# Placed dummies, u in its own bank, x copied by two engines and a last group with tokens on partitions, in a sketched attention with an MLP behind it

## The chip, the core and the metric

The kernel runs on one core of a Trainium2 chip. The core has TensorE (PE, matmuls; PEld is its weight loads), VectorE (DVE), ScalarE (ACT), GpSimd (POOL) and SyncE (SP), each with its own instruction stream, joined by semaphores. DMAs are issued from the streams of SyncE and ScalarE. The metric is device time in microseconds (us) of one execution, as the median of several; lower is better. The profile of one execution gives its span, from the first to the last instruction, on which all times below are counted.

## What is computed

```python
# q, k, v: (4, 4, 1088, 32), S1, S2: (8, 32), w_in: (128, 2048), w_out: (2048, 128)
def phi(x):                                   # 64 features of a token
    a = einsum('rd,bhsd->bhsr', S1, x)
    b = einsum('rd,bhsd->bhsr', S2, x)
    return einsum('bhsi,bhsj->bhsij', a, b).reshape(..., 64)
q_p, k_p = phi(q), phi(k)
kv  = einsum('bhsf,bhsd->bhfd', k_p, v)
z   = sum(k_p, axis=2)
num = einsum('bhsf,bhfd->bhsd', q_p, kv)
den = einsum('bhsf,bhf->bhs', q_p, z)[..., None] + 1e-06
x   = (num / den).transpose(0, 2, 1, 3).reshape(4352, 128)
h   = x @ w_in
out = (h - tanh(h)) @ w_out                   # (4352, 128)
```

There is no softmax: the sums over the keys of a batch (kv and z) are small matrices, and each token of q is weighed with them. Since h − tanh(h) is linear in its first part, the kernel computes the output as x @ (w_in @ w_out) + tanh(−h) @ w_out, with w_in @ w_out kept as two bf16 matrices, whi and wlo.

## The kernel before, in words

A small planner (class Program) takes all operations with their reads, writes, costs and priorities, and writes out one order for each engine; semaphore waits follow from it. An operation of the MLP has a due time (`due`, from FIRST, TILE, EARLY; matmuls by w_out LAG later), and earlier operations get theirs by counting back with the costs stretched by STRETCH. So constants such as LAG, TILE, STRETCH, HELD, HOT and LATE change nothing but the order. For the opening (batch 0), the dictionary LINE fixes the order of the named operations on each engine (lines 52 to 59), and other operations fall between them where the planner puts them.

**Opening, batch 0.** Two tiny DMAs bring S1 and S2, ScalarE's queue brings k, SyncE's the first half of q and v. `warm` offers dummies, which multiply a tile of zeros into PSUM bank 6: 36 (BURN) of 128 columns and 60 of 512; the planner puts them where TensorE has nothing ready, until the matmuls of line 840. `sketch` (L569) spreads S; VectorE makes from it the masked weights wkm (L572), wqb's first part wab (L576) and wab2 (L580). k is transposed on VectorE in 32x32 blocks into kT (L600, four pieces) and projected (keys0, keys1, L618); ScalarE copies the projections (kab, L628), and VectorE and GpSimd multiply them into features wk (L650, L636). `spread` (L585) and s2c (L588) prepare the second sketch; `gram` (L666), gm (L695) and `fold` (L704) make a small matrix, from which VectorE writes wqb's second part wu (L715). q of the first 512 tokens (chunk a) is projected in two steps: `qab` with the first 16 columns of wqb and `qu` with the last 8, both into PSUM bank 1 (L773). ScalarE copies qab's part (ab, L798). VectorE multiplies u with ab (au, L802), reduces it to the denominator (dn, L805), inverts it (rd, L808), scales (an, L810), multiplies out the features (qp, L819; the other half on GpSimd, L814), and transposes them (qpT, L825, two pieces). `sums` (L676) are kv, copied to kvz (L728), turned (L734) and copied to ndw (L739); `nd0` and `nd1` (L840) weigh qpT with ndw into banks 4 to 7, and line 854 copies the result, cast to bf16, to xT.

**Weights.** w_in comes in four DMAs, issued by SyncE once the first kab is there, w_out in two, once wu is there. They are cast to bf16 on ScalarE (w_in 0 to 2) and GpSimd (w_in 3 and w_out). w_in is transposed on TensorE (L875) and multiplied with w_out (L889) for whi and wlo.

**The other chunks.** The remaining 576 tokens of batch 0 (chunk c, projection `qc`) and then batches 1 to 3, of 1088 tokens each, go the same way (L784, L707 in place of L773, L704), between the MLP's matmuls. Loads of batch 1 wait for GATE1, those of later batches for GATES of the batch before.

**MLP.** The tokens are cut into eight groups of 512 and one of 256. For each of 16 blocks of w_in, a matmul (L918) writes h of the group, transposed, into one of PSUM banks 4 to 6; ScalarE writes tanh(−h) to one of 40 slots of tt (L921); a matmul by w_out (L929) adds it up in bank 7, with whi and wlo (L910) in the same sum. VectorE transposes the sum in 32x32 blocks into osb (L936), and four DMAs, one for each 32 columns of the output, write it out in rows of 128 bytes (L945), from SyncE; in the last group two of them from ScalarE.

## Time and profile before

| what | value |
|---|---|
| time, median of 3 runs | 108.56 us (108.46 to 108.84) |
| time of the profiled execution | 108.72 us |
| its span | 106.9 us |
| TensorE matmuls busy | 99.4 us (93%) |
| ScalarE busy | 76.5 us (72%), of it 70.2 us tanh |
| VectorE, GpSimd busy | 61.1 us, 23.9 us |
| first matmul of the MLP (L918) | 17.61 us |
| x of batch 3 there, last run of tanh begins | 80.89 us |
| transpose of the last group | 103.74 us |

Busy times are sums over instructions; matmuls are pipelined, so their busy time holds some overlap. The chain of waits follows back, from the last instruction, what released each step, or the instruction ahead of it on its engine. A timeline line gives start, length, engine, line, operation, and the idle time before it with what ended it.

### The profile page before, as it was taken

To read this page: it belongs to the slowest core of one execution; us is meant where nothing else is said; L and a number is where in the kernel's file an instruction comes from. 1 tells how busy PE (TensorE), PEld (TensorE's weight loads), DVE (VectorE), ACT (ScalarE), POOL (GpSimd) and SP (SyncE) were. 2 spreads that over 40 slices of the span, in tenths; PEclk is the share of its full clock that TensorE was granted. 3 is DMA by queue.
4 is the path that set the end of the run, shared out by engine and by line. 5 is a ranking of instruction groups with operands and counts; after the bars stand their busy time and mean duration, and the time that the engine had idled before them with its cause. 6 is when DMAs were issued, how large, how long until landed. Compare 5 with 4: busy or idle time off the path is not lost.

```text
span 106.9 us, 3548 instructions
## 1 busy us (share of the span) xinstructions
PE 99.4 (93%) x1534; PEld 56.6 (53%) x1552; DVE 61.1 (57%) x119; ACT 76.5 (72%) x160; POOL 23.9 (22%) x34
## 2 busy tenths in 40 slices
PE   5999999999999999999999999999999999999970
PEld 5967657445566544536465446544644344345650
DVE  3672797996389987734999914486935100200210
ACT  3012174997168964996978698679777999999960
POOL 5517076400531600620430005308000000000000
PEclk9999999999999999999999999999999999999997
DMA  3987899920024793600189613300132041023153
GB/s 58 348 209 213 287 291 294 297 63 0 6 35 69 238 323 74 96 3 6 13 326 266 94 38 47 51 6 0 23 49 32 0 71 27 6 42 57 17 84 49
DMA packets 25247, 11.24 MB, mean 105 GB/s; under 512 B 18832, under 2 KB 23440, under 8 KB 25232
## 3 DMA queue, kind: packets, MB, share of 16 engines
q1 hardware_dynamic: 24400, 10.40, 40.3%
q10 hardware_dynamic: 832, 0.62, 2.2%
q8 instruction: 12, 0.20, 0.8%
q14 instruction: 3, 0.02, 0.1%
HBM read 8.79 MB, written 2.23 MB: 103 GB/s over the span
## 4 chain that ended last, share of the span: by engine, by line
PE 81%; ACT 12%; issue 3%; DVE 1%; DVEq 0%
PE ps L929 23%; PE ps L918 23%; ACT tt L921 11%; PE ps L565 7%; PE ps L840 6%; PE ps L910 4%; PE ps L618 4%; PE ps L784 4%; PE ps L676 3%; PE ps L773 2%; DVE osb L936 1%; PE ps L875 1%; PE ps L666 1%; PE ps L889 1%; PE ps L734 1%
## 5 line engine op out<-in xcount | busy, mean ns | idle before, releaser
L921 ACT ACTIVATE tt<-ps 128x512 bf16<-128x512 f32 (+1 forms) x144 | 70.2, 594 | 11.6 <-PE ps L918 6.5
L918 PE MATMUL ps<-xT,w_in 128*128 128x512 bf16 (+1 forms) x135 | 47.5, 367 | 1.5 <-issue 1.0
L929 PE MATMUL ps<-tt,w_out 128*128 128x512 bf16 (+1 forms) x139 | 44.4, 367 | 0.3 <-issue 0.3
L918 PEld LDWEIGHTS ps<-xT,w_in 128*128 128x128 bf16 x144 | 13.4, 97 | 16.3 <-ACT tt L921 5.4
L929 PEld LDWEIGHTS ps<-tt,w_out 128*128 128x128 bf16 x144 | 13.9, 98 | 14.1 <-issue 1.2
L936 DVE STREAM_TRANSPOSE osb<-ps 128x512 f32<-128x512 f32 (+1 forms) x9 | 6.2, 684 | 23.1 <-PE ps L929 23.1
L636 POOL TENSOR_TENSOR wk<-kab 128x512 f32<-128x512 f32 (+1 forms) x8 | 9.4, 1180 | 28.5 <-ACT kab L628 28.0
L814 POOL TENSOR_TENSOR qp<-an,ab 128x1152 f32<-128x1152 f32 (+2 forms) x5 | 8.9, 1778 | 19.4 <-DVE an L810 19.4
L825 DVE STREAM_TRANSPOSE qpT<-qp 128x1152 f32<-128x1152 f32 (+2 forms) x10 | 11.0, 1112 | 0.1
L565 PE MATMUL ps<-wz 128*128 128x128 bf16 (+1 forms) x47 | 7.4, 334 | 1.4 <-DVE hmask L532 1.2
L840 PE MATMUL ps<-qpT,ndw 32*32 32x288 f32 (+3 forms) x320 | 7.0, 352 | 0.0
L854 DVE CAST xT<-ps 128x512 bf16<-128x512 f32 x8 | 5.2, 687 | 3.1 <-PE ps L840 3.0
L650 DVE TENSOR_TENSOR wk<-ps,kab 128x512 f32<-128x512 f32 (+1 forms) x8 | 5.8, 740 | 0.7 <-ACT kab L628 0.7
L600 DVE STREAM_TRANSPOSE kT<-kraw 128x256 f32<-128x256 f32 (+3 forms) x10 | 5.7, 600 | 0.6 <-DMA kraw<-in_k_dram 0.6
L565 PEld LDWEIGHTS ps<-wz 128*128 128x128 bf16 x50 | 4.9, 135 | 2.0 <-DVE hmask L532 1.2
L628 ACT COPY kab<-ps 128x320 f32<-128x320 f32 (+1 forms) x5 | 2.1, 419 | 5.4 <-PE ps L618 5.4
L618 PEld LDWEIGHTS ps<-wkm,kT 128*64 128x64 f32 x144 | 4.8, 141 | 2.0 <-DVE xT L854 0.8
L618 PE MATMUL ps<-wkm,kT 128*64 128x64 f32 x144 | 5.4, 229 | 0.3 <-issue 0.3
L819 DVE TENSOR_TENSOR qp<-an,ps 128x1152 f32<-128x1152 f32 (+2 forms) x5 | 5.6, 1114 | 0.2
L840 PEld LDWEIGHTS ps<-qpT,ndw 32*32 32x32 f32 x320 | 4.0, 103 | 3.2 <-DVE qpT L825 1.0
L746 DVE STREAM_TRANSPOSE qT<-qraw 128x512 f32<-128x512 f32 (+3 forms) x9 | 5.6, 651 | 0.0
L798 DVE COPY ab<-ps 128x576 f32<-128x576 f32 x3 | 2.3, 758 | 5.2 <-PE ps L784 5.2
(72 smaller groups left out, 71.1 us busy)
## 6 DMA issues: line engine op xcount, KB each, us to landing
kraw<-in_k_dram SPq DMA_DIRECT2D x3, 544.0 KB, 4.1
qraw<-in_q_dram SPq DMA_DIRECT2D x3, 544.0 KB, 5.6
out_dram<-osb SPq DMA_DIRECT2D x20, 64.0 KB, 2.0
w_in_f<-in_moe_w_in_dram SPq DMA_DIRECT2D x4, 256.0 KB, 4.3
w_out_f<-in_moe_w_out_dram SPq DMA_DIRECT2D x2, 512.0 KB, 5.4
vx<-in_v_dram SPq DMA_DIRECT2D x6, 144.0 KB, 5.4
vx<-in_v_dram SPq DMA_DIRECT2D x6, 128.0 KB, 5.4
vx<-in_v_dram SPq DMA_DIRECT2D x6, 64.0 KB, 2.8
```

Source lines behind the costliest of these rows:

```text
L565: P.op("tensor", cost, lambda e: e.matmul(ps[:, 6, 0:cols], wz[:, 0:128], wz[:, 0:cols], start=True, stop=True), r=[("wz",)], prio=prio)
L600: P.op("vector", dve(hi - lo), lambda e, cb=cb, t0=t0, n=n, lo=lo, hi=hi: e.transpose(out=kT[i][:, t0:t0 + n, cb:cb + 2, :], in_=kraw[i][: ...
L618: ins = e.matmul(dst[64 * c:64 * c + 64, :, :, t - t0, :], kT[i][:, t, 2 * c:2 * c + 2, :].rearrange("p c j -> p (c j)"), wkm[:, :, :, :]. ...
L636: P.op("gpsimd", pool(64 * n), lambda e, t0=t0, t1=t1, n=n, ab_=ab_: e.tensor_tensor(out=wk[:, 1, t0:t1, :, :].rearrange("p t h (i j) -> p ...
L650: P.op("vector", dve(64 * n), lambda e, t0=t0, t1=t1, n=n, a_ps=a_ps, b_sb=b_sb: e.tensor_tensor(out=wk[:, 0, t0:t1, :, :].rearrange("p t ...
L814: P.op("gpsimd", pool(64 * n), lambda e: e.tensor_tensor(out=qp[u][:, 1, 0:64 * n].rearrange("p (n i j) -> p n i j", i=R, j=R), in0=an[u][ ...
L825: c.t_op = P.op("vector", dve(64 * n), lambda e, r=r: e.transpose(out=qpT[u][:, r, 0:64 * n], in_=qp[u][:, r, 0:64 * n]), r=[("qp", u, r)] ...
L840: ins = e.matmul(ps[32 * h:32 * h + 32, k0 + s, 0:32 * own[s]], ndw[b % 2][32 * s:32 * s + 32, y, 32 * h:32 * h + 32], src, start=(y == 0) ...
L918: P.op("tensor", pe(n), lambda e, jb=jb, bk=bk: e.matmul(bk[:, 0:n], w_in[:, 128 * jb:128 * jb + 128], xT[:, t0:t0 + n], start=True, stop= ...
L921: P.op("scalar", act(n), lambda e, ts=ts, bk=bk: e.activation(out=tt[:, ts, 0:n], in_=bk[:, 0:n], func=AF.Tanh, scale=-1.0), r=[kb], w=[(" ...
L929: P.op("tensor", pe(n), lambda e, jb=jb, ts=ts: e.matmul(acc[:, 0:n], w_out[:, jb, :], tt[:, ts, 0:n], start=(jb == 0 and not g), stop=(jb ...
L936: P.op("vector", dve(n), lambda e: e.transpose(out=osb[u][:, 0:n], in_=acc[:, 0:n]), r=[ka], w=[("osb", u)], want=due(NJB) + LAG)
```

## The change

The diff, cut to its core. Planner constants whose lines are left out: BIAS (0 to 10), HOT (4000 to 3900), HELD (ScalarE added), STRETCH (TensorE and ScalarE 1.8 to 1.3, GpSimd 1.6 to 1).

```diff
-LAG = 8000
-TILE = 760
+LAG = 6000
+TILE = 680
-COPY_K = ("scalar", "scalar", "vector")
+COPY_K = ("scalar", "vector", "vector")
-COPY_Z = "vector"
+COPY_Z = "scalar"
-W_PRIO = 22
-BURN = 36
+W_PRIO = 26
-X_A = "vector"
-ORD = 3
+X_A = "vector", "scalar"
+ORD = 2
-C_ENG = "scalar", "scalar", "scalar", "gpsimd"
-GATES = "an", "an", "an"
+C_ENG = "scalar", "scalar", "gpsimd", "gpsimd"
+GATES = "an", "wu", "x"
-GATE1 = "qpT", 0, 1
+GATE1 = "xT", 0, 0
+FILLS = 29, 3, 0, 1, 0, 0, 4, 4
 LINE = {
-    "tensor": ("sketch", "keys0", "keys1", "spread", "gram", "qab", "fold", "qu", "sums0", "sums4", "turn", "nd0", "nd1", "qc"),
-    "vector": (("kT", 0, 0, 0), ("kT", 0, 0, 2), ("wkm",), ("wab",), ("kT", 0, 1, 0), ("kT", 0, 1, 2), ("qT", 0, 0),
-               ("wk", 0, 0), ("s2c",), ("gm",), ("wu", 0), ("wk", 0, 1), ("au", 0), ("dn", 0), ("rd", 0), ("an", 0), ("qp", 0, 0),
-               ("qpT", 0, 0), ("qpT", 0, 1), ("qT", 0, 1), ("qT", 0, 3), ("xT", 0, 0)),
-    "gpsimd": (("wk", 1, 0), ("wk", 1, 1), ("qp", 0, 1), ("w_in", 3), ("w_out", 0), ("w_out", 1)),
-    "scalar": (("kab", 0, 0), ("kab", 0, 1), ("ab", 0), ("kvz",), ("ndw", 0), ("w_in", 0), ("w_in", 1), ("w_in", 2)),
+    "tensor": ("fill0", "sketch", "fill1", "keys0", "keys1", "spread", "fill3", "gram", "qab0", "fold", "qab1", "qu",
+               "sums0", "sums4", "fill6", "turn", "fill7", "nd0", "nd1", "qc"),
+    "vector": (("kT", 0, 0, 0), ("kT", 0, 0, 2), ("wkm",), ("kT", 0, 1, 0), ("kT", 0, 1, 2), ("wab",), ("qT", 0, 0),
+               ("wk", 0, 0), ("s2c",), ("gm",), ("wab2",), ("wu", 0), ("wk", 0, 1), ("au", 0), ("dn", 0), ("rd", 0), ("an", 0), ("qp", 0, 0),
+               ("qpT", 0, 0), ("qpT", 0, 1), ("qT", 0, 1), ("xT", 0, 0), ("qT", 0, 3)),
+    "gpsimd": (("wk", 1, 0), ("wk", 1, 1), ("qp", 0, 1), ("w_in", 2), ("w_in", 3), ("w_out", 0), ("w_out", 1)),
+    "scalar": (("kab", 0, 0), ("kab", 0, 1), ("ab", 0), ("kvz",), ("ndw", 0), ("w_in", 0), ("w_in", 1), ("xT", 0, 2)),
 }
-LATE = 400
+LATE = 60
...
+    def warm():
+        for x, n in enumerate(FILLS):
+            for _ in range(n):
+                P.op("tensor", 54, lambda e: e.matmul(
+                    ps[:, 6, 0:128], wz[:, 0:128], wz[:, 0:128], start=True, stop=True), r=[("wz",)], name=f"fill{x}")
...
         def fold(e):
...
-                if b == 0:
-                    ins = e.matmul(ps[:, gb, 64:80], s2c[:, :, :].rearrange("p h d -> p (h d)"), g_, start=(y == 0), stop=(y == 1))
-                    continue
                 for h in range(H):
                     ins = e.matmul(ps[32 * h:32 * h + 32, gb, 64:80], s2c[:, h, :], g_, start=(y == 0), stop=(y == 1),
                                    tile_position=(0, 32 * h))
...
+        ku = 5
...
+                        if early and y0:
+                            dst = ps[64 * s:64 * s + 64, ku, 32 * t:32 * t + 32].rearrange("p (h y) -> p h y", h=4)
...
         if early:
-            P.op("tensor", 117 * nt + 10, project(0, 16), r=[("wab",)] + need, w=kb, mode="k", ni=8 * nt, name="qab")
+            for x in range(2):
+                P.op("tensor", 58 * nt + 5, project(0, 16, range(2 * x, 2 * x + 2)), r=[("wab",)] + need, w=kb, mode="k", ni=4 * nt, name=f"qab{x}")
...
+        pu, ub = pv[:, :, :, 16:24], kb
         if early:
-            c.second = P.op("tensor", 117 * nt + 10, project(16, 24), r=[("wab",), ("wu", b)] + need, w=kb, mode="k", ni=8 * nt, name="qu")
+            pu, ub = ps[:, ku, 0:16 * n].rearrange("p (n r x) -> p r n x", r=2, x=8), [bank[ku]]
+            c.second = P.op("tensor", 117 * nt + 10, project(16, 24), r=[("wab",), ("wu", b)] + need, w=ub, mode="k", ni=8 * nt, name="qu")
...
-        cuts = [(0, tm // 2), (tm // 2, tm)] if tm > 4 else [(0, tm)]
+        cuts = [(0, tm // 2), (tm // 2, tm)] if tm != 4 or c.x == 0 else [(0, tm)]
         for a, z in cuts:
-            eng = X_A if c.x == 0 else "vector"
+            eng = X_A[a > 0] if c.x == 0 else "vector"
...
+        last = g == len(groups) - 1
+        blocks = [(ps[:, 6 - x, 0:128], bank[6 - x], 128 * x) for x in range(n // 128)] if last else []
+        pairs = [(jb, jb + 1) for jb in range(0, NJB - 2, 2)] + [(NJB - 2,), (NJB - 1,)] if last else [(jb,) for jb in range(NJB)]
+        for x, js in enumerate(pairs):
+            if last:
+                bk, kb = ps[:, x % 5, :], bank[x % 5]
...
+            P.op("scalar", act(m), lambda e, ts=ts, bk=bk, m=m: e.activation(
+                out=tt[:, ts, 0:m], in_=bk[:, 0:m], func=AF.Tanh, scale=-1.0),
...
+                if last:
+                    for o_, ko, at in blocks:
+                        P.op("tensor", pe(128), lambda e, jb=jb, ts=ts, o_=o_, at=n * y + at: e.matmul(
+                            o_, tt[:, ts, at:at + 128], w_out[:, jb, :], start=False, stop=jb == NJB - 1),
...
+        for x, (o_, ko, at) in enumerate(blocks):
+            eng, q = (("vector", "sync"), ("scalar", "scalar"))[x % 2]
+            P.op(eng, (act if x % 2 else dve)(128), lambda e, x=x, o_=o_: (e.copy if x % 2 else e.tensor_copy)(
+                osbt[:, 128 * x:128 * x + 128], o_), r=[ko], w=[("osbt", x)], want=due(NJB) + LAG)
...
+                out=ob[b, :, c:c + 4, :].rearrange("j c e -> c j e"),
+                in_=osbt[:, 128 * x:128 * x + 128]), r=[("osbt", x)], sem=f"out{u}t{x}", want=due(NJB) + LAG + 3000)
```

In words: the dummies are a fixed number at fixed places of TensorE's opening order (29 ahead of sketch, 3 ahead of keys0, 1 ahead of gram, 4 ahead of turn, 4 ahead of nd0), all of 128 columns. qab is two halves with fold between them, fold is made of eight tiled matmuls, and qu writes bank 5. The x of chunk a is copied in two halves, one by VectorE and one by ScalarE, and the cast of w_in 2 goes to GpSimd. In the last group two blocks of h share a bank and one tanh; the matmuls by w_out take the tanh tile as the stationary operand, so that the output has tokens on partitions, in two blocks of 128 in banks 6 and 5; these are copied by VectorE and ScalarE and written by one DMA each, from SyncE and ScalarE, in rows of 512 bytes. The planner orders all operations outside LINE anew.

## Prediction

> **What bounds the kernel now.** I read the page first, then the chain of waits over the first 18 us, then the waits of TensorE behind them, the timelines of ScalarE and SyncE, and last the stretches of the final 7 us.
>
> ```profile
> PE 99.4 (93%) x1534; PEld 56.6 (53%) x1552; DVE 61.1 (57%) x119; ACT 76.5 (72%) x160; POOL 23.9 (22%) x34
> ```
>
> TensorE fills the span. What it fills it with differs by stage. The chain over 0 to 18 us (start, length, what) shows the opening:
>
> ```profile
> 1.19 3.17 PE ps L565 x28
> 4.36 0.54 PE ps L569 x2
> 4.89 1.39 PE ps L565 x9
> 6.28 0.76 PE ps L618 x16
> 7.05 0.25 issue
> 7.30 0.80 PE ps L618 x20
> 8.10 0.41 PE ps L585 x2
> 8.51 0.54 PE ps L565 x2
> 9.05 0.31 PE ps L666 x20
> 9.36 0.61 PE ps L773 x16
> 9.98 0.55 PE ps L704 x4
> 10.53 0.07 issue
> 10.59 0.59 PE ps L565 x2
> 11.18 0.59 PE ps L773 x16
> ...
> 14.75 1.18 PE ps L840 x64
> 15.93 0.55 PE ps L875 x8
> 16.48 0.98 PE ps L773 x20
> 17.45 0.16 issue
> 17.61 0.59 PE ps L918 x2
> ```
>
> L565 are dummies: they multiply zeros and only occupy the engine. Those after 4.89 stand in the chain between real steps, each time after the input of the next step was there. From 17.61, where the MLP begins, there is next to no gap: between 17 and 104 us the waits of TensorE's matmuls sum to 2.3 us (1.0, 0.5, 0.3, 0.3 and 0.2). So the MLP stage, 17.61 to 103.65, is 86 us of TensorE work, and the time is set by when that work starts, how long it is, and what follows it. ScalarE has gaps, but not at the end (timeline of ScalarE; idle before in brackets):
>
> ```profile
> 41.70 1.58 ACT L921 ACTIVATE tt<-ps 128x512 bf16<-128x512 f32 x3 [2.61 <-PE ps L918]
> ...
> 80.89 18.04 ACT L921 ACTIVATE tt<-ps 128x512 bf16<-128x512 f32 x37 [1.42 <-PE ps L918]
> ```
>
> From 80.89 to 103.30 tanh runs without a pause, beside a full TensorE. These two lines are the limits that a shift has to respect. After the last matmul (stretches; last columns are granted clock, DMA share, GB/s):
>
> ```profile
> 104.00:104.50 0.50, 0.00 (x0) 0.00 (x0) 0.19 (x1) 0.00 (x0) 0.00 (x0) 1.00 0.00 0
> 104.50:105.00 0.50, 0.00 (x0) 0.00 (x0) 0.00 (x0) 0.00 (x0) 0.00 (x0) 1.00 0.00 0
> 105.00:105.50 0.50, 0.00 (x0) 0.00 (x0) 0.00 (x0) 0.00 (x0) 0.00 (x0) 1.00 0.78 114
> ```
>
> That tail of 3.25 us has a 0.45 us transpose at 103.74, two issues on each of SyncE and ScalarE (0.88 us from 104.22), and 1.1 us of data at 114 to 138 GB/s.
>
> **The opening, part by part.** *Before the sketch:* 29 dummies for 28, at 3.17/28 = 0.11 us: +0.11. *Sketch to keys0:* the mask multiply wkm ended at 5.16, yet keys0 began at 6.28 behind nine dummies (1.39 us). Three remain (0.33 us), so wkm decides: 5.16 + 0.11 + 0.08 for the hand-over = 5.35, or −0.93 with the extra dummy counted. *keys0 to keys1:* the 0.25 us is one 512-column dummy (its record is missing); gone, −0.25. keys1 needs the second pair of kT transposes, now ahead of wab on VectorE and done near 5.95, under keys0. Against that, keys0 runs 1 us earlier, when matmuls may still be slow: its first six took 0.38 us, the next eight 0.23. I take +0.10; bounds 0 and +0.8 (both key blocks at the slow pace). *gram:* its input kab ended at 8.57; two dummies held it to 9.05. With one 0.06 us dummy it starts near 8.65: −0.40. *gram to au:* before, gram at 9.05, au at 11.82, 2.77 us. Now: gram 0.31, gm 0.25 with hand-over, during which qab0 (half of 0.61) runs; fold at +0.62 as tiled matmuls, 0.25 by the later batches' row (L707 x16) for 0.55; wu ends at +1.14; qab1 runs under it; qu from +1.21, 0.59. u has its own bank, so qu no longer waits for the copy of ab (10.03 to 10.40). VectorE issues wab2 (0.25) between gm and wu, and the second wk (0.81) after wu ends near +1.9, which sets au at +1.92: −0.85. *au to the end of nd1:* 11.82 to 15.93 is VectorE's chain au, dn, rd, an, qp and two qpT; the dummies there (now 4 and 4 of 128 columns for 2 and 4 of 512) lie under it; only nd0 started 0.2 us late, half of it hidden under the second qpT: −0.05. Sum to the end of nd1: −0.93 −0.25 +0.10 −0.40 −0.85 −0.05 = −2.4, so 13.55.
>
> *x copied by two engines:* the 128x512 cast took 0.69 (16.03 to 16.72). The 128x256 halves take 0.37 on ScalarE (row of 128x256 copies) and about 0.41 on VectorE (0.69 − 256 columns at 0.96 per ns). Before, this lay under a w_in transpose (0.55) and qc (0.98). Now qc has to wait for the last qT transpose, put behind x, so the transpose alone (it needs casts 0 and 1 of w_in, behind ndw at 11.7) covers the 0.5 us until x. Uncovered it costs 0.45. TensorE's stream after nd1 is the same work, so all of the −2.4 passes on as long as work is there. I take −2.2, holding back 0.2 for the order of list scheduling; bounds −2.9 and −0.6.
>
> *Casts and loads:* w_in 2 moves from ScalarE (0.62) to GpSimd (0.61), which delays w_in 3 and w_out there by 0.6; GpSimd is free from 11.9 in the new order (its qp took 13.22 to 14.29) and waited 1.2 us on w_out anyway. w_in's four DMAs hang on the first kab and w_out's two on wu: issued about 1 and 2 us earlier, into DMA stretches of 0.39 to 0.8 share. w_out landed at 15.5 and 17.2; even there the first 2.5 us of the MLP have qc, two transposes and five L918 to do: 0. The six loads of batch 1 (SyncE, 15.23 on) now wait for x's first half instead of the second qpT: about 14.0, 1.2 earlier, not 2.4. Only this can bite (rival B).
>
> **The middle.** Same matmuls, other order, by new constants. ScalarE loses three copies of 0.43 and gets three of 0.37; VectorE the reverse, beside 23.1 us of waiting for L929 alone. In later batches the load of q waits for wu and that of v for x, in SyncE's order with the outputs behind them; v landed 4.8 us after issue, far ahead of sums. I put it at 0; bounds −1.0 (half of the 2.3 us of waits, and some of the pace lost to tanh) and +1.5 (the 2.61 us gap, partly passed to TensorE).
>
> **The last group.** Tanh: fourteen of 16 halves go pairwise, 7 x 0.50 + 2 x 0.30 = 4.1 us for 16 x 0.30 = 4.8. TensorE: 36 matmuls of 128 columns at 0.89/16 = 0.056 (product row, L889) = 2.0 for 18 x 0.11 = 2.0: equal. With TensorE the bound I take 0; −0.7 if tanh is. Then two copies side by side: 0.25 on VectorE (128x128 row, L893), about 0.27 on ScalarE, for 0.45: −0.18. One issue per queue for two: −0.42. Data: 1,024 packets of 128 bytes become 256 of 512. If the packet count set the 1.1 us, it goes to 0.3; if bytes did, it stays: I take −0.35, nearest to the opening's loads, whose longer rows moved at 208 to 376 GB/s. Tail −0.95; bounds −0.2 and −1.4.
> The Trainium skill, DMA: Bandwidth & Descriptors, section Specifications, gives 512 B as the shortest transfer at line rate, with a read-modify-write below it. By that rule the data would take about 0.4 us, an estimate from that page, and the tail −1.3; the 138 GB/s of the 128-byte rows agrees.
>
> **Sum.** −2.2 + 0 − 0.95 = −3.15 on the profiled execution's 108.72 us (span 106.9, 1.8 around it), 0.16 above the median 108.56: 105.57, forecast 105.5.
>
> **Rivals.** *A, the opening runs at half pace.* 28 dummies took 0.113 us each, the product's matmuls 0.056, so TensorE speeds up somewhere near 6.5. With fewer dummies it may come one period later, and keys1, gram, fold, qu and half of qab (2.2 us on the path) nearly double, less what VectorE covers: +1.6, 107.1. For: dummies after the sketch fall from 9 to 3. Against: the 29 before it stay, and real matmuls move in. Chance 0.12.
> The Trainium skill, TensorE: Matmul & The Clock Gate, section Part 1: The HAM clock gate, says that about 3.4 us of sustained work lift the clock from half to full and that an idle window lowers it. By it, short gaps leave the pace alone; the row of 0.50 granted clock after the last matmul agrees, while the opening's rows show 1.00 even for the slow dummies.
> *B, batch 1 comes too late.* Its loads move by 1.2 only, and L918 of its tokens started at 41.40, just behind x at 41.2, so TensorE had no slack. If batch 1 gains only the 1.2, a hole of about 1.1 opens: 106.6; with the 2.61 us gap of ScalarE passed on as well, 107.5. Against: VectorE idled 1.5 us at 26 to 28, waiting for TensorE. Chance 0.14.
> *C, slower.* L929 is due 6 instead of 8 us behind, so attention work yields to it and the x of batch 3 comes late. From there tanh is the bound: 22.4 us now, 21.7 with the pairs, then 4.5 to the end. It beats the gain when tanh's last run starts after 82.5 (now 80.89); at 83.5 it gives 109.7. Against: tanh idles 11.6 us in all. Chance 0.09.
> *D, the change doesn't do what it says:* the wait for the small load of S or kT holds the opening where the dummies stood; 0.5 gained there, and the tail: 107.3. Against: kT ended at 4.51 and 5.96. Chance 0.05.
>
> **Numbers.** Forecast 0.60, its own range 104.3 to 106.4 (middle −1.0, tail −0.4 more; +0.9 from the opening). With A, B and D, which are faster too, that makes 0.91, of which 0.03 go to ends of B and D within 0.3% of now (about what a measurement of this kernel can tell): faster 0.88, same 0.03; slower is C, 0.09. Leaving out C and the far ends, the range is 104.3 to 107.3.
>
> **What would show it.** keys0 near 5.35, qu ended near 9.4, nd1 near 13.6, the first L918 near 14.1 in the chain; ab copied before qu ends; one out issue on each queue in the tail and the data in under 0.8 us; TensorE's waits after 14 us still near 2 us. Wrong would be: key matmuls at double length up to 9 us (A), a gap of TensorE before L918 of batch 1 (B), tanh's last run starting after 81 (C).

## The result: a third of the forecast gain

The changed kernel takes 107.68 us (median of 18 runs, 106.81 to 111.09) against 108.51 us for the kernel before on the same chip (18 runs, 107.52 to 110.01). The ratio is 0.9915, 95% interval [0.9887, 0.9943], so some 0.9 us less. The forecast was 105.5 us in a range of 104.3 to 107.3: the sign was right, the size was not. The profiled execution of the changed kernel took 107.03 us with a span of 105.2, against 108.72 and 106.9 before, so this pair differs by 1.7 us. The remaining 0.8 us is spread between executions: the profiled one before lies 0.2 above its median, the profiled one after 0.65 below. Runs more than 1.5% above the fastest of the same kernel (four of the 18 after, one of the 18 before) are left out of all ratios, and seven of the experiments' profiled executions are such runs, so what only they show is not what the ratios rest on.

The profile after, first the busy line of the page:

```profile
PE 96.1 (91%) x1557; PEld 56.1 (53%) x1573; DVE 61.0 (58%) x119; ACT 75.5 (72%) x154; POOL 24.5 (23%) x35
```

TensorE still fills the span, with 3.3 us less busy time. The chain of waits of the kernel after, over 0 to 18 us (start, length, what; L568 dummies, L572 sketch, L621 keys, L883 the transpose of w_in, L932 the MLP's matmul by w_in):

```profile
1.19 3.27 PE ps L568 x29
4.46 0.54 PE ps L572 x2
5.00 0.41 PE ps L568 x3
5.41 0.64 PE ps L621 x16
...
7.34 5.90 DMA w_in_f<-in_moe_w_in_dram
13.24 0.05 issue
13.29 0.62 POOL w_in L519
...
14.03 0.62 POOL w_in L519
14.66 0.05 issue
14.70 0.62 PE ps L883 x8
15.32 0.05 issue
15.38 0.59 PE ps L932 x2
```

keys0 begins at 5.41 instead of 6.28, as forecast (5.35). But from 7.34 on the chain is no longer the attention of batch 0: it is the load of w_in, its casts on GpSimd and its transpose. The attention ends earlier, and the weights become the next thing to wait for. The timeline of TensorE of the same kernel shows the attention's own path (L679 sums, L734 turn, L848 nd0 and nd1; idle before in brackets):

```profile
9.23 1.21 PE L679 MATMUL ps<-wk,vx 128*32 128x64 f32 x72
10.38 0.40 PE L568 MATMUL ps<-wz 128*128 128x128 bf16 x4
10.94 0.44 PE L734 MATMUL ps<-ident,kvz 128*128 128x128 f32 x2 [0.16 <-ACT kvz L728]
11.21 0.28 PE L568 MATMUL ps<-wz 128*128 128x128 bf16 x2
12.48 0.27 PE L568 MATMUL ps<-wz 128*128 128x128 bf16 x2 [0.99 <-issue]
12.69 1.15 PE L848 MATMUL ps<-qpT,ndw 32*32 32x128 f32 x64
```

sums begin at 9.23 (before 11.70) and nd1 ends at 13.84 (before 15.93; forecast 13.55). Between the second and the third dummy ahead of nd0 there is a stop of 0.99 us in which TensorE waits for no other engine. Then the two halves of x, from the timelines of VectorE, ScalarE and TensorE:

```profile
13.88 0.42 DVE L862 CAST xT<-ps 128x256 bf16<-128x256 f32 x1 [0.76 <-PE ps L848]
...
14.34 0.37 ACT L862 CAST xT<-ps 128x256 bf16<-128x256 f32 x1 [1.12 <-DVE xT L862]
...
14.70 0.62 PE L883 MATMUL ps<-identb,w_in 128*128 128x128 bf16 x8 [0.31 <-POOL w_in L519]
```

The two halves do not run side by side: ScalarE's waits for VectorE's.

The end, from the timeline of all engines of the kernel after (SPq and ACTq are DMA issues):

```profile
101.05 0.29 DVE L969 COPY osbt<-ps 128x128 f32<-128x128 f32 x1 [2.08 <-PE ps L955]
101.10 0.27 ACT L969 COPY osbt<-ps 128x128 f32<-128x128 f32 x1 [0.38 <-PE ps L955]
101.39 0.65 SPq L973 DMA_DIRECT2D out_dram<-osbt  x1
101.40 1.30 ACTq L973 DMA_DIRECT2D out_dram<-osbt  x1
```

and the stretch in which the last data move, before and after (last columns: granted clock, DMA share, GB/s):

```profile
105.00:106.10 1.10, 0.00 (x0) 0.00 (x0) 0.00 (x0) 0.00 (x0) 0.00 (x0) 0.76 0.82 119
```

```profile
102.60:104.50 1.90, 0.00 (x0) 0.00 (x0) 0.00 (x0) 0.00 (x0) 0.00 (x0) 0.93 0.25 69
103.00:103.50 0.50, 0.00 (x0) 0.00 (x0) 0.00 (x0) 0.00 (x0) 0.00 (x0) 1.00 0.28 76
```

Both move the same 128 KB. Before, they took 1.1 us at a mean share of 0.82 of the 16 engines; now they take 1.8 us, and the share is 0.28, that is four to five engines. The span ends 4.15 us after the first copy begins; before, it was 3.2 us after the transpose began at 103.74. From the last matmul to the span's end, the tail has become 0.9 us longer, where the forecast had it 0.95 shorter.

The parts of the profiled pair, in us:

| stretch | before | after | difference | forecast |
|---|---|---|---|---|
| start to nd1's end | 15.93 | 13.84 | −2.1 | −2.4 |
| nd1's end to the last matmul's end | 87.7 | 87.2 | −0.5 | 0.2 |
| last matmul to the span's end | 3.25 | 4.15 | +0.9 | −0.95 |
| span | 106.9 | 105.2 | −1.7 | −3.15 |

(0.2 in the second row is what the forecast held back of the opening's 2.4.)

### The profile page after: what moved, and what is told of

The parts are those of the page before. It is cut to its first block, busy times and chain, and to the rows that moved or that the text cites. A ratio compares the mean times of both kernels' runs of the same rounds, so it can differ in the third digit from the quotient of the medians.

```text
span 105.2 us, 3584 instructions
## 1 busy us (share of the span) xinstructions
PE 96.1 (91%) x1557; PEld 56.1 (53%) x1573; DVE 61.0 (58%) x119; ACT 75.5 (72%) x154; POOL 24.5 (23%) x35
## 4 chain that ended last, share of the span: by engine, by line
PE 72%; ACT 13%; DMA 6%; issue 2%; DVE 1%; POOL 1%; SPq 1%; POOLq 0%
PE ps L932 22%; PE ps L959 21%; ACT tt L940 12%; DMA w_in_f<-in_moe_w_in_dram 6%; PE ps L848 5%; PE ps L789 4%; PE ps L621 4%; PE ps L568 4%; PE ps L918 3%; PE ps L679 2%; PE ps L955 2%; POOL w_in L519 1%; PE ps L669 1%; PE ps L778 1%; PE ps L897 1%
## 5 line engine op out<-in xcount | busy, mean ns | idle before, releaser
L940 ACT ACTIVATE tt<-ps 128x512 bf16<-128x512 f32 (+1 forms) x137 | 69.4, 620 | 14.6 <-PE ps L932 4.4
L932 PE MATMUL ps<-xT,w_in 128*128 128x512 bf16 (+1 forms) x130 | 43.6, 367 | 1.3 <-issue 1.0
L959 PE MATMUL ps<-tt,w_out 128*128 128x512 bf16 x126 | 41.9, 379 | 0.7 <-issue 0.6
L932 PEld LDWEIGHTS ps<-xT,w_in 128*128 128x128 bf16 x144 | 13.2, 97 | 15.6 <-ACT tt L940 3.3
L959 PEld LDWEIGHTS ps<-tt,w_out 128*128 128x128 bf16 x128 | 12.5, 98 | 12.9 <-issue 0.4
L978 DVE STREAM_TRANSPOSE osb<-ps 128x512 f32<-128x512 f32 x8 | 5.7, 708 | 19.7 <-PE ps L959 19.7
L568 PE MATMUL ps<-wz 128*128 128x128 bf16 x41 | 4.9, 292 | 2.2 <-DVE hmask L534 1.2
L848 PE MATMUL ps<-qpT,ndw 32*32 32x288 f32 (+3 forms) x320 | 6.9, 352 | 0.0
L862 DVE CAST xT<-ps 128x512 bf16<-128x512 f32 (+1 forms) x8 | 4.9, 643 | 2.7 <-PE ps L848 2.7
L621 PEld LDWEIGHTS ps<-wkm,kT 128*64 128x64 f32 x144 | 4.6, 138 | 1.6 <-DVE xT L862 0.8
L848 PEld LDWEIGHTS ps<-qpT,ndw 32*32 32x32 f32 x320 | 4.0, 103 | 2.6 <-DVE ndw L739 0.8
L568 PEld LDWEIGHTS ps<-wz 128*128 128x128 bf16 x41 | 3.9, 135 | 2.6 <-DVE hmask L534 1.2
L621 PE MATMUL ps<-wkm,kT 128*64 128x64 f32 x144 | 5.3, 225 | 0.0
L679 PEld LDWEIGHTS ps<-wk,vx 128*32 128x32 f32 x288 | 4.2, 110 | 1.3 <-issue 1.3
```

What stands on the lines that cost most here:

```text
L568: P.op("tensor", 54, lambda e: e.matmul(ps[:, 6, 0:128], wz[:, 0:128], wz[:, 0:128], start=True, stop=True), r=[("wz",)], name=f"fill{x}")
L621: ins = e.matmul(dst[64 * c:64 * c + 64, :, :, t - t0, :], kT[i][:, t, 2 * c:2 * c + 2, :].rearrange("p c j -> p (c j)"), wkm[:, :, :, :]. ...
L679: ins = e.matmul(ps[32 * h:32 * h + 32, 2, 0:64], vx[i][:, h, t, :], wk[:, h // 2, t, h % 2, :], start=(t == 0), stop=(t == 8), tile_posit ...
L848: ins = e.matmul(ps[32 * h:32 * h + 32, k0 + s, 0:32 * own[s]], ndw[b % 2][32 * s:32 * s + 32, y, 32 * h:32 * h + 32], src, start=(y == 0) ...
L932: o = P.op("tensor", pe(n), lambda e, jb=jb, bk=bk, y=y: e.matmul(bk[:, n * y:n * y + n], w_in[:, 128 * jb:128 * jb + 128], xT[:, t0:t0 + ...
L940: P.op("scalar", act(m), lambda e, ts=ts, bk=bk, m=m: e.activation(out=tt[:, ts, 0:m], in_=bk[:, 0:m], func=AF.Tanh, scale=-1.0), r=[kb], ...
```

## The experiments

All ratios are to the kernel before, run on the same chip.

### The tail: which dimension of a DMA is the outermost

The last DMAs write 128 partitions of 512 bytes, but with the partitions split into four groups as the first dimension: 4 x 32 x 128. The first experiment has x of the last group written in another order of tokens, so that the DMA's first dimension is 32; five small VectorE copies do it, earlier in the kernel. The second leaves x alone and cuts each DMA in four, each with 32 partitions first.

```diff
-                out=ob[b, :, c:c + 4, :].rearrange("j c e -> c j e"),
+                out=ob[b, :, c:c + 4, :],
```

> The changed kernel, but the 256 columns of x of the last group stand in the order (j, c) instead of (c, j), so that each of the two last DMAs has 32 x 4 rows instead of 4 x 32; same bytes, same rows of 512 bytes, same engines and orders, five small copies of x in place of two. Theory 1 (the outermost dimension of 4 lets only a quarter of the DMA engines work: share 0.28 and 76 GB/s after 103 us): the last data move at a share near 0.9 and end before 103.0, the time from the last matmul to the end of the span falls from 4.15 us to about 2.4, and the kernel takes 0.969 to 0.977 of the time before. Rival 1 (rows of 512 bytes out of 128 partitions, or the outputs of the group before that still run until 102.5, make the end long whatever the order of the dimensions): 4.15 stays within 0.3, 0.99 of the time before.

Measured: 106.5 us, ratio 0.9805 [0.9771, 0.984], 1.1 points below the changed kernel and faster than both. Its issues and stretches:

```profile
101.90 0.64 SPq L982 DMA_DIRECT2D out_dram<-osbt  x1
101.93 0.66 ACTq L982 DMA_DIRECT2D out_dram<-osbt  x1
```

```profile
103.10:103.80 0.70, 0.00 (x0) 0.00 (x0) 0.00 (x0) 0.00 (x0) 0.00 (x0) 0.85 0.67 187
103.30:103.40 0.10, 0.00 (x0) 0.00 (x0) 0.00 (x0) 0.00 (x0) 0.00 (x0) 1.00 1.01 287
```

Same bytes, same rows of 512 bytes, same two queues: the data take 0.63 us instead of 1.77, at a share of up to 1.01, and ScalarE's issue takes 0.66 us instead of 1.30. The span ends 3.0 us after the copies begin, 1.1 less than in the changed kernel, which is nearly the whole gain. So the cause is the order of the DMA's dimensions.

The expectation asked for more, 2.4 us and a ratio of at most 0.977. The missing 0.6 us does not lie in the rows. A tenth of a microsecond of the kernel before, with its rows of 128 bytes on all engines, shows it:

```profile
105.70:105.80 0.10, 0.00 (x0) 0.00 (x0) 0.00 (x0) 0.00 (x0) 0.00 (x0) 0.50 0.96 141
```

At nearly the same share, 512-byte rows move 287 GB/s and 128-byte rows 141. Read from the packets in the traces, the tail is made up like this (us, counted from the start of the transpose or of the first copy):

| part of the tail | before | after | first experiment | forecast |
|---|---|---|---|---|
| transpose or copies, to the first issue | 0.48 | 0.34 | 0.32 | 0.30 |
| first issue to the first data | 0.82 | 1.29 | 1.29 | 0.40 |
| the data | 1.07 | 1.77 | 0.63 | 0.72 |
| last data to the span's end | 0.82 | 0.78 | 0.79 | 0.82 |

(The forecast is the column before with the prediction's −0.18, −0.42 and −0.35.) With all engines at work, the longer rows save what the forecast had for them. What the forecast still misses is the second line: one DMA of 128 partitions reaches its first data 0.5 us later than the first of several with 32 partitions.
The Trainium skill, DMA: Bandwidth & Descriptors, section Why a DMA increments its semaphore by 16 and not by 1, says that a DMA is spread over the largest number of engines, up to 16, that divides the slowest dimension of both sides, which makes four here; the share of 0.28 agrees, and so does the jump to a share of 1.01 at 32.

```diff
+            for y in range(4):
+                q = ("sync", "scalar")[(x + y) % 2]
+                P.op(q, 65, lambda e, b=b, c=lo // 32 + y, x=x, y=y: e.dma_start(
+                    out=ob[b, :, c, :], in_=osbt[32 * y:32 * y + 32, 128 * x:128 * x + 128]),
```

> The changed kernel, but each of the two last DMAs cut into four of 32 partitions (outermost dimension 32), four issues in a row on each of SyncE and ScalarE; rows of 512 bytes as before. Theory 1: all DMA engines work (share over 0.5 while the data move), each issue takes about 0.44 us, so the last is issued near 103.1 and lands 1.6 later: end of the span 3.4 to 3.7 us after the last matmul, 0.980 to 0.988 of the time before. Rival 1: the rows themselves are slow, and with more issues the end is at 4.15 us or later, 0.99 or more.

Measured: 106.81 us, ratio 0.9861 [0.9817, 0.9905], as expected: better than four engines, worse than one DMA with 32 as its first dimension, since the four issues on each queue now take 1.7 to 1.8 us; the span ends 3.7 us after the copies begin:

```profile
101.62 1.73 SPq L975 DMA_DIRECT2D out_dram<-osbt  x4
101.63 1.80 ACTq L975 DMA_DIRECT2D out_dram<-osbt  x4
```

Third, the old last group (transposed output, four DMAs of 128-byte rows, single tanhs) with everything else of the change:

```diff
-        last = g == len(groups) - 1
+        last = False
```

> The changed kernel with the last group as it was before (transposed output in rows of 128 bytes, sixteen tanh of 256 columns, four DMAs on two queues); the order up to the last third of the kernel is that of the changed one. Theory 1: the tail goes back to 3.25 us from 4.15, while the end of the matmuls comes 0 to 0.7 later (tanh needs 4.8 for 4.1 us); 0.977 to 0.987 of the time before, so the new last group as it stands costs 0.2 to 0.9. Rival 1 says the same of the tail. Rival 2 (what the last group saves in tanh is worth more than what its DMAs cost): 0.992 or more.

Measured: 108.45 us, ratio 0.9952 [0.9917, 0.9986]. That is the value of rival 2, and theory 1 failed: the new last group, even with its slow DMAs, does not cost. Its tail is 0.9 us longer than the old one, so the rest of it (tanh in pairs, copies side by side) must gain at least as much, which the forecast had at 0 and 0.18. The profiles have 0.7 to 1.0 us of it ahead of the tail (below, under the middle), but this kernel's (109.0 us) holds a wait of 2.2 us for w_in that has to be taken off, and the interval is 0.7 points wide, so how much it gains is not settled.

### The opening: what the placed dummies and the banks are worth

The order of the change with the dummies of before behind the same first 29, so 51 in all instead of 41 (put places so many dummies of so many columns ahead of the named step):

```diff
+        fills = ('fill1', 'fill3', 'fill6', 'fill7')
+        order["tensor"] = [o for o in order["tensor"] if o.name not in fills]
...
+        put('keys0', 8, 128)
+        put('keys0', 1, 512)
+        put('keys1', 1, 512)
+        put('gram', 2, 512)
+        put('qu', 3, 512)
+        put('turn', 3, 512)
+        put('nd0', 4, 512)
```

> The changed kernel in its own order, with the dummies after sketch as the kernel before had them and where it had them: 8 of 128 and 1 of 512 columns before keys0, 1 of 512 before keys1, 2 before gram, 3 before qu, 3 before turn, 4 before nd0. Theory 2 (the dummies stood in the path of the opening, as the prediction has it): nd1 ends 1.4 to 2.0 us later than the 13.84 of the changed kernel, near 15.5, and most of it reaches the end: 1.003 to 1.01 of the time before. Rival 3 (the weights that land at 11.7 to 17.4 us pace the start of the MLP, not the dummies): nd1 moves as much but the first tanh (15.58) and the end by under 0.5; 0.992 to 0.997.

Measured: 110.01 us, ratio 1.0086 [1.0044, 1.0129]: 1.7 points worse than the change, worse even than before. The chain of its profiled execution (111.18 us) over 11 to 16 us, and nd1 from its timeline of TensorE (L697 sums, L866 nd0 and nd1):

```profile
11.47 0.59 PE ps L796 x16
12.06 1.13 PE ps L697 x69
13.19 1.92 issue
15.12 0.30 PE ps L697 x3
```

```profile
17.18 1.15 PE L866 MATMUL ps<-qpT,ndw 32*32 32x128 f32 x64
```

qu ends at 12.06, no earlier than before (11.77), where the changed kernel has it at 9.3: up to there the dummies take back the opening's whole gain. But nd1 ends at 18.33, not near the expected 15.5, and part of that is a stop of 1.92 us in the middle of 72 equal matmuls, where no semaphore is waited for. So the 1.7 points hold both, and no run tells them apart. It is the stop of the changed kernel at another place: there it came 2 dummies before nd0, here 3 sums before their end. Between these two places lie 3 sums, 4 dummies, 2 turns and 2 dummies, 11 matmuls, and this kernel has 11 dummies more ahead of its sums (44 for 33). So it sits at a fixed number in TensorE's instruction stream: in all seven traces that have it, 222 weight loads and about as many matmuls stand ahead of its end (the 505th instruction of the expectations adds 63 that the kernel's planner counts ahead of them). Ahead of each such stop one packet of 16 KB moves on the queue that the profile lists as q8, instruction (10.11 to 11.03 in the changed kernel, 12.79 to 13.73 here), and TensorE resumes 1.2 to 1.5 us after its end. All this fits TensorE waiting for its own code; no run tested it by itself. In six profiled executions of kernels with the change's count of instructions the stop was 0.44, 0.79, 0.99, 1.14, 1.40 and 1.50 us. In the kernel before the same number falls to nd0, whose input is not there before 14.5 anyway.
The Trainium skill, Runtime: NRT & Kernel Launch, section Instruction fetch mechanics, has code fetched in blocks of 16 KiB, 256 instructions, beside execution, at a cost that is mostly hidden; the block's size agrees with the packet, the hiding does not hold here.

u back in bank 1, so that qu waits for the copy of ab:

```diff
+        named["qu"].deps.add(named[("ab", 0)])
...
-        ku = 5
+        ku = 1
```

> The changed kernel in its own order, but u stands in bank 1 beside qab's columns, as before, so that qu waits for ScalarE's copy of ab. Theory 2 (the opening is one chain, and each wait in it reaches the end): the copy of ab (8.76 to 9.13 in the changed kernel) ends before qu may start, so qu moves from 8.64 to about 9.2, au and nd1 with it by 0.5 us, and the end by 0.3 to 0.5: 0.994 to 0.997 of the time before, for 0.9915. Rival 3 (the weights that land from 11.7 to 13.6 us pace the start of the MLP): qu moves as much, the end by 0.2 or less: 0.990 to 0.993.

Measured: 107.89 us, ratio 0.994 [0.9911, 0.9969], at the edge of theory 2's range, with rival 3's inside the interval, and not to be told from the change's 0.9915. The timeline of TensorE in its profiled execution (109.4 us):

```profile
9.28 0.66 PE L780 MATMUL ps<-wqb,qT 128*64 128x32 f32 x16 [0.56 <-ACT ab L806]
...
12.56 0.28 PE L570 MATMUL ps<-wz 128*128 128x128 bf16 x2 [0.44 <-issue]
12.77 1.23 PE L850 MATMUL ps<-qpT,ndw 32*32 32x128 f32 x64
```

The wait that the new bank removes is real, 0.56 us, and sums begin 0.64 later (9.87 for 9.23). But nd1 ends at 14.00 for 13.84, not the 0.5 later of theory 2, because the stop ends where it ended before (12.56 for 12.48): one late thing hides behind the other.

No dummies at all:

```diff
+        fills = ('fill0', 'fill1', 'fill2', 'fill3', 'fill4', 'fill5', 'fill6', 'fill7')
+        order["tensor"] = [o for o in order["tensor"] if o.name not in fills]
```

> The changed kernel in its own order without any dummy, those ahead of sketch included. Theory 4 (rival A of the prediction: without sustained work before it the opening runs at half pace): the twenty key matmuls of keys1 take 1.3 us or more for 0.8, nd1 ends 1 us or more later than 13.84, and the time is 1.0 or more of the time before. Rival 4 (the pace follows from the time since the start, or the DMA of S holds sketch at the same place): sketch starts no later than 4.4, keys1 at 0.8, nd1 within 0.4 of 13.84, 0.988 to 0.995.

Measured: 108.73 us, ratio 1.0014 [0.9968, 1.0061]. S lands at 3.86 and the sketch begins then, 0.5 us earlier than with 29 dummies (4.39 by the timeline), but (chain, L632 keys, L690 sums):

```profile
4.82 2.38 PE ps L632 x36
...
10.79 1.90 PE ps L690 x72
```

36 matmuls of the keys take 2.38 us for 1.45, the 72 sums 1.90 for 1.21, and nd1 ends at 15.27 for 13.84. This is rival A, TensorE at a slower pace until about 12 us, as theory 4 has it, and it takes away the whole gain of the change.

Since the sketch's input is there at 3.86, 24 dummies should do:

```diff
+        fills = ('fill0',)
+        order["tensor"] = [o for o in order["tensor"] if o.name not in fills]
...
+        put('sketch', 24, 128)
```

> The kernel after with 24 dummies ahead of the sketch in place of 29. In the kernel without the first dummies the sketch started at 3.86, when its load landed; with 29 it started at 4.46, behind the last dummy. Theory 1 (the 29 hold the sketch, and the opening is a chain from the sketch on): the sketch starts 0.3 to 0.5 us earlier, keys0 at about 4.9 to 5.0 and nd1 ends 0.3 to 0.5 us earlier, ratio to before .987 to .990. Rival (what bounds nd0 is the stop of TensorE at its 505th instruction, which ends some 4.4 us after the block before it was begun, or the pace of TensorE falls with fewer dummies): nd1's end moves by 0.2 us at most, ratio .990 to .994.

Measured: ratio 0.9901 [0.9857, 0.9944] (median 108.0): nothing that can be told from the change. In the profiled execution (108.77 us) the opening did gain. From its timeline of TensorE (L580 dummies, L860 nd0 and nd1), and from its chain:

```profile
10.77 0.39 PE L580 MATMUL ps<-wz 128*128 128x128 bf16 x4
11.82 1.26 PE L860 MATMUL ps<-qpT,ndw 32*32 32x128 f32 x64 [0.66 <-DVE qpT L845]
```

```profile
8.61 11.21 DMA w_out_f<-in_moe_w_out_dram
```

nd1 ends at 13.08, 0.76 earlier than after: the sketch's start carries 0.37 of it (VectorE's qpT at 11.05 for 11.42), and no stop shows: the place lies five matmuls further on, inside nd0, and the packet of code ended at 10.55, over 1.2 us before nd0 began. But w_out, issued at 8.61, landed only at 19.82, and TensorE then waited 1.7 us for the cast of w_in and 1.0 for that of w_out. In this execution the next limit is the weights' loads. In the changed kernel, too, they were issued earlier and the last of them came no earlier: w_in 1 us earlier, landing after 3.0 to 6.1 us for 3.6 to 4.7; w_out 2 us earlier, after 7.1 to 8.3 us for 4.7 to 6.0.

To see whether the stop moves with the instructions' number, 14 dummies of 256 columns and one of 128 for the 29, the same time with 14 weight loads and 14 matmuls fewer:

```diff
+        put('sketch', 14, 256)
+        put('sketch', 1, 128)
```

> The kernel after with its first 29 dummies of 128 columns replaced by 14 of 256 and one of 128: the same TensorE time, 28 TensorE instructions (14 weight loads and 14 matmuls) fewer. Theory 1 (the stop ahead of nd0 is at an instruction's number, where the next block of 256 is not there yet): it comes 28 instructions later in the program, so behind the start of nd0 and not in the dummies ahead of it, right after a 16 KB transfer of the instruction queue. Rival (a wait of that place for something that no row shows): it stays between the second and the third dummy ahead of nd0 and ends at about 12.5.

One run, 109.02 us. It tells nothing of the stop, since another thing happened (timeline of TensorE, L634 keys, L692 sums):

```profile
5.36 2.34 PE L634 MATMUL ps<-wkm,kT 128*64 128x64 f32 x36
...
11.44 2.15 PE L692 MATMUL ps<-wk,vx 128*32 128x64 f32 x72
```

This execution had the slow pace of the kernel without dummies until 13.5 us, sums at 2.15 us, and nd1 ended at 16.13. Nothing stopped: the packet of code had ended at 13.06, and nd0 began at 14.98.

The first experiment and the 24 dummies together (both edits as shown):

> The first experiment (the last group's x written so that the last transfers' slowest dimension is 32) together with 24 dummies ahead of the sketch. If the sketch's earlier start comes through to the end: ratio to before .976 to .979, some 0.3 to 0.5 us under the first experiment's. If it does not: .979 to .983, as the first experiment alone.

Measured: ratio 0.9803 [0.9738, 0.9868] (median 107.11, six runs): as the first experiment alone, 0.9805. Its profiled execution (107.67 us), too, had the slow opening (timeline of TensorE):

```profile
4.82 2.19 PE L633 MATMUL ps<-wkm,kT 128*64 128x64 f32 x36
...
10.75 2.15 PE L691 MATMUL ps<-wk,vx 128*32 128x64 f32 x72
```

with nd1's end at 15.77. With the same 24 dummies the profiled execution above ran its keys in 1.48 us. So rival A is no matter of yes or no. The granted clock of the stretches does not help here: it reads 1.00 in all these openings, but it is a mean over the trace's records of the clock and counts 1.00 where there is none, and the first record, of the full clock, comes at another time in each execution:

| kernel | full clock recorded from | 36 key matmuls | 72 sums | nd1's end |
|---|---|---|---|---|
| 24 dummies | 4.56 | 1.48 | 1.21 | 13.08 |
| after | 5.26 | 1.45 | 1.21 | 13.84 |
| first experiment and x by banks (below) | 6.87 | 1.94 | 1.21 | 15.52 |
| no dummies | 12.25 | 2.38 | 1.91 | 15.27 |
| 15 wide dummies | 13.62 | 2.34 | 2.15 | 16.13 |
| first experiment and 24 dummies | 13.98 | 2.19 | 2.15 | 15.77 |

The slow matmuls stand ahead of that record, the fast ones behind it. (nd1's 15.52 also holds a stop of 1.50 us.) In the kernel before, the record comes at 6.58, inside keys0. Of ten profiled executions with the change's order and the first dummies (24 or 29, or 15 as long), eight have it by 6.9 us and two at 13.6 and 14.0; in these two nd1's end came 2.3 and 1.9 us later than after.
The Trainium skill, TensorE: Matmul & The Clock Gate, section Part 1: The HAM clock gate, says that the window of about 3.4 us that decides the pace runs freely, so that the number of slow matmuls varies from run to run; the rows of the two kernels with 24 dummies agree, and the records between two changes of the clock last 3.41 us or whole multiples of it (6.83 and 92.16, for instance). Why in two executions the full clock came only after some 14 us, with TensorE busy from 1.2 us on, no row shows.

### x on two engines

VectorE and ScalarE copy banks 4 and 5, and 6 and 7, without the wait, and the second w_in transpose goes behind the first three matmuls of the MLP:

```diff
+        line.remove(turns[1])
+        line.insert(line.index(first[2]) + 1, turns[1])
...
+        x[("xT", 0, 2)].deps.discard(x[("xT", 0, 0)])
...
+                ps[:, k0 + a:k0 + z, 0:128].rearrange("p s (t j) -> p s t j", j=32)),
```

> The changed kernel in its own order, with two edits at the start of the MLP: the two engines copy x by banks (VectorE banks 4 and 5, ScalarE 6 and 7), so that neither waits for the other, and the second transpose of w_in stands behind the first three matmuls by w_in, not ahead of them. Rival 3 (ScalarE's half of x waiting for VectorE's, and the cast of the last quarter of w_in ahead of the first matmul by w_in, hold the start of the MLP): the first tanh comes at 14.7 for 15.58, and since tanh and TensorE both start earlier the end moves by 0.3 to 0.6 us: 0.986 to 0.989 of the time before. Theory 2 (TensorE's work after nd1 is the same and its waits there are only 0.3 us): the first tanh moves as much, the end by 0.3 or less: 0.989 to 0.992.

Measured: ratio 0.9898 [0.9824, 0.9972], nothing that so wide an interval can tell from 0.9915. Its profiled execution (110.93 us) had the second part of k late by 2.5 us and gives no reading of the MLP's start. Together with the first experiment (both edits as shown):

> Both: the last group's x in the order (j, c), which gave 0.9805, and the two edits at the start of the MLP. If the two gains add, this is the sum: 0.975 to 0.978 by rival 3, 0.978 to 0.981 by theory 2; the tail stays 3.0 us after the last matmul.

Measured: ratio 0.9796 [0.9735, 0.9857], as the first experiment alone. Its profiled execution (107.87 us) shows that the edit does what it should. From the timelines of VectorE and ScalarE:

```profile
15.56 0.42 DVE L871 CAST xT<-ps 128x256 bf16<-128x256 f32 x1 [1.86 <-PE ps L855]
...
15.56 0.37 ACT L871 CAST xT<-ps 128x256 bf16<-128x256 f32 x1 [2.23 <-PE ps L855]
```

The halves run side by side, x is there 0.46 us behind nd1's end (15.52) instead of 0.87, and the first matmul of the MLP begins at 16.28, 0.76 behind it instead of 1.54. The same execution shows one more thing that a stop can cost, in the stretches around the one of 1.50 us (granted clock third from the end):

```profile
12.00:14.00 2.00, 0.50 (x18) 0.40 (x26) 1.70 (x3) 1.33 (x3) 0.60 (x2) 0.92 1.05 314
14.00:16.00 2.00, 2.00 (x70) 1.52 (x54) 0.44 (x2) 0.37 (x1) 1.02 (x2) 0.50 1.12 279
```

With TensorE busy for 0.5 us of two, the granted clock fell to 0.50, for 3.41 us from 13.69 on, and the 64 matmuls of nd0 and nd1 took 1.82 us for 1.15. In the profiled execution with the late k it fell the same way, behind the 2.5 us without matmuls.

Whether x's wait costs anything at the end is not settled; 0.4 us would be at the edge of what these intervals show.

### The middle: the new order by itself

The kernel before with only the seven planner constants of the change:

```diff
-LAG = 8000
-TILE = 760
+LAG = 6000
+TILE = 680
-BIAS = 0
+BIAS = 10
-STRETCH = {"tensor": 1.8, "scalar": 1.8, "vector": 1.3, "gpsimd": 1.6, "sync": 1}
+STRETCH = {"tensor": 1.3, "scalar": 1.3, "vector": 1.3, "gpsimd": 1, "sync": 1}
-HELD = "vector",
+HELD = "vector", "scalar"
-HOT = 4000
-LATE = 400
+HOT = 3900
+LATE = 60
```

> The kernel before with nothing of the change but the planner's seven constants (LAG, TILE, BIAS, STRETCH, HELD, HOT, LATE). Theory 1 (the prediction's: the middle's new order is worth nothing): ratio .997 to 1.003. Rival 1 (the constants carry the 0.5 us that the middle gained): .993 to .997. Rival 2 (they fit the new opening alone, and cost with the old one): over 1.003.

Measured: 109.05 us, ratio 1.0042 [1.0006, 1.0079]: a small loss, +0.45 us. In its profiled execution nd1 ends at 15.80 and the last transpose begins at 104.05, 88.25 us, against 87.81 before: the loss is in the middle. So with the old opening the constants bring nothing. How the same stretch, nd1's end to the first copy or transpose of the last output, stands in the profiles: with the old last group 87.81 (before), 88.25 (here) and 90.14 in the kernel of the change with the old last group, of which 2.2 are a wait for w_in, so 87.9; with the new one 87.21 (after) and 86.8 to 87.7 in eight others without late weights, with a median of 86.9. By these profiles the −0.5 of the table goes with the last group rather than with the order; only one of them, the 87.9, has the new order with the old last group.

## Why the prediction was off, step by step

**The tail failed.** The step "Tail −0.95; bounds −0.2 and −1.4" measured +0.9, which is 1.85 us of the gap, and more than the whole miss of the profiled pair (1.45). The copies held (0.29 for 0.45). Two terms came out with the wrong sign. "One issue per queue for two: −0.42": ScalarE's one issue took 1.30 us where its two had taken 0.88, and the first data came 1.29 us after the first issue instead of 0.82. "Data: 1,024 packets of 128 bytes become 256 of 512", −0.35: the data took 0.7 us longer, on a quarter of the engines. The forecast priced the length of a row and the number of DMAs, and did not ask how many engines carry the transfer, although the rows of before showed a share of 0.78 and more and the diff showed an access pattern with a dimension of four ahead. For rows of 512 bytes on all engines its price was about right: the first experiment's data took 0.63 us against 1.07 before, −0.44. With the dimensions in that order the issue took 0.66 us, and the kernel 106.5 us, inside the forecast's range. Both bounds were gains, so the range left no room for what came.

**The opening held.** Sketch 4.46 by both; keys0 5.35 forecast, 5.41 measured; no gap within the keys; qu's end 9.4 and 9.3; nd1's end 13.55 and 13.84. The 0.3 is the stop ahead of nd0: nd1 ended 0.73 after the second qpT in the experiment with 24 dummies, so without the stop it would have been at 12.72 + 0.73 = 13.45. The forecast's −0.05 for "au to the end of nd1" was in error only there. In rival A the prediction takes the clock's 1.00 beside slow dummies for a measurement; the trace of before has no record of the clock until 6.58, which is where the prediction itself puts the change of pace (near 6.5).

**x by two engines.** "Halves 0.37 and 0.41" are the measured lengths, but one after the other: x was ready at 14.71, 0.87 behind nd1 instead of 0.46. The planner's rule lets a reader of a PSUM bank wait for a reader of the same bank on another engine, and both halves read banks 4 to 7. The first matmul of the MLP, forecast at 14.1, came at 15.38; 0.6 of that is the second w_in transpose, which went ahead of it instead of behind.

**Casts and loads, 0.** They cost 0.3 us of TensorE's wait in the changed kernel (the second w_in transpose waits for the cast on GpSimd). The step expected an earlier landing from an earlier issue and asked only in passing whether the weights are there "even there", at the old landing times; these were the right ones (the last of w_in at 13.94 for 13.52, of w_out at 17.39 for 17.22). In the profiles of three experiments, executions of 108.8 to 109.4 us, TensorE waited 2.2 to 2.7 us for the casts.

**The middle and the last group, 0 and 0.** They came to −0.5, within the bounds. The forecast named "−0.7 if tanh is" the bound. The last run of tanh goes without a pause in both kernels, so from its start tanh was the bound:

```profile
78.62 22.10 ACT L940 ACTIVATE tt<-ps 128x512 bf16<-128x512 f32 x45 [1.36 <-PE ps L848]
```

It lasts 22.1 us for 22.4 (80.89 to 103.30), so 0.3 of the 0.5 is gained in it and the other 0.2 before it begins.

**The rivals.** C did not come: tanh's last run began at 78.62, not after 82.5. B did not come: no gap of TensorE over 0.2 us stands ahead of the MLP of batch 1. A came in some executions, with 1.9 and 2.3 us where 1.6 was forecast, and the number of dummies alone does not decide it: of two executions with the same 24, one had it and one had not. How much of the spread between executions comes from the pace, how much from the stop and from late weights, is open, since most runs have no trace.

## What to carry to other kernels

Read a DMA's dimensions from the outside in before pricing its rows, and compare the share of engines in the stretch that is to be changed: four groups ahead of 32 partitions cost this kernel 1.1%, and writing the tokens in another order got it back. Choose stretches no longer than the transfer: in half a microsecond, from 103.00 to 103.50, the first experiment's burst at up to 287 GB/s reads as 139. Ask of a column what it shows where nothing was recorded. When an opening is made shorter, ask of each load whether it lands earlier or is only issued earlier, and, where the engine's code may still be arriving, at which instruction the stop falls. A few tenths gained under a wait that stays (a bank, a copy, five dummies) do not reach the end.

## What the runs showed of the hardware

- Two DMAs of 128 x 512 bytes, each written as 4 x 32 x 128, moved at a share of 0.28 and 76 GB/s (the whole 128 KB in 1.77 us); as 32 x 4 x 128 at a share of up to 1.01 and 287 GB/s (0.63 us). ScalarE's issue took 1.30 us for the first form and 0.66 for the second.
- At nearly the same share, rows of 128 bytes wrote 141 GB/s (share 0.96) and rows of 512 bytes 287 GB/s (share 1.01).
- In seven profiled executions TensorE stopped for 0.44 to 1.92 us behind the same 222 weight loads, until 1.2 to 1.5 us after a packet of 16 KB on the instruction queue, while loads kept the DMA engines at a share of 0.8 to 1.1.
- The full clock of TensorE was recorded from 4.56 to 6.87 us in eight of ten profiled openings with the same dummies, and from 13.62 and 13.98 in two; until then matmuls took up to 1.8 times as long (72 in 2.15 us for 1.21). Behind a stop of 1.50 us, and behind a wait of 2.48 us, the recorded clock fell to 0.50.
